# A fused attention, MLP and expert kernel: third expert chosen from six tiles, seventh tile turned on TensorE, a fourth staging buffer early

## The chip, the cores and the metric

The kernel runs on one core of one Trainium2 chip. The metric is the device time of one execution in microseconds. The kernel before took 443.18 us in the median of three runs (439.34 to 447.48). The engines are TensorE (PE, with its weight loads PEld), VectorE (DVE), ScalarE (ACT), GpSimd (POOL) and SyncE (SP), which issues most DMAs. Each works its own instructions in a fixed order.

## The reference, cut to what matters

Three stages follow each other: causal attention with a position bias, a dense MLP with `h * cos(h)`, and a mixture of eight experts with one expert per token and a capacity.

```python
x = attn_out.transpose(0, 2, 1, 3).reshape(1152, 512)   # 2 x 576 tokens
h = x @ w_in                    # 512 x 2048
x = (h * np.cos(h)) @ w_out     # 2048 x 512
logits = x @ w_gate             # 8 experts
expert_idx = np.argmax(logits, axis=1)
gate_w = probs[np.arange(N), expert_idx]          # softmax
for i in range(N):              # rows in order, up to capacity 288 each
    e = expert_idx[i]
    if counts[e] < capacity: disp[e, counts[e]] = x[i]; counts[e] += 1; keep[i] = True
h = np.maximum(np.einsum('ecd,edf->ecf', disp, w1), 0.0)   # 512 x 1024
y = np.einsum('ecf,efd->ecd', h, w2)                       # 1024 x 512
out[i] = gate_w[i] * y[expert_idx[i], pos[i]]     # kept rows, else zero
```

## The kernel before, in words

The 1152 tokens are nine tiles of 128, numbered 0 to 8. Products run as sums of fp16 parts: every operand is kept as a high and a low half, and three matmuls (high by high, high by low, low by high) make one.

The second half of the MLP (`l2_mm`, L862) first does tiles 0 to 4 together (`l2_wide`), then tiles 5 to 8 one after the other (`l2`), 48 matmuls each. When a tile is done, `l2_end` writes its two halves to `row` by ACT (L853) and DVE (L854). Each tile is then routed. `route_a` turns it: tiles below `NDT` by a DMA transpose that SP issues (L890), the others by four fp32 transposes on TensorE (L895), for which ACT first copies the tile to `xq` (L851) and afterwards copies the turned tile back (L897). `route_b` computes the logits (L912 in fp16, L909 in fp32 for the tiles turned on TensorE), takes the argmax on DVE (one-hot `roh`, L926), finds each row's place by a matmul with `tri` (L931), adds to the counts `cnt` (L941) and scatters the rows to `disp` in DRAM with an indirect DMA from POOL (L942). `l2r` interleaves all this with the matmuls of tiles 5 to 8.

The expert layer does not take the experts in order. The first is fixed. `partial` picks the next, the one with the most rows so far, and reads its number into SP's registers: once after tile `PTILE` = 4 (counts of five tiles), once after tile `HTILE` = 7 (counts of eight). The first two experts start with their first 144 rows (`HEAD`, at most; those of tiles 0 to 6), for which `hook` issues two row reads each: a transposing one to `eX` (L1008) and a small one to `eM` (L1015). After tile 8, `counts` sorts the remaining experts on DVE (L1184 to L1201) and chooses one of four tables of sizes:

```python
SIZES = (
    (64, 56, 184, 168, 152, 144, 128, 120),
    (72, 64, 192, 168, 152, 144, 136, 128),
    (88, 88, 200, 176, 160, 152, 136, 128),
    (128, 96, 216, 192, 176, 152, 144, 144),
)
```

A row must hold the rest of the first two experts, all rows of the third, and the five others by size; the program branches on that. The executed table here is the first.

Expert weights come as 64 loads of 512 KB (L964 for w1, L968 for w2; eight per expert) into staging buffers `ws`, three of them until the MLP is over and four from then on, taken in turn. Each is split by ACT (high half, L648) and then DVE (low half, L649); when DVE is done the buffer may be loaded again. `expert` computes eight steps of 12 matmuls (L1039), each into a PSUM bank of the rotation s, pt, mm with two buffers each, evicted to `eH` by ACT (L1041) and DVE (L1042), and then the second layer (L1061) and the scatter to the output (L1048). The first steps of the first expert stand beside the routing of tile 8.

What sets the order: the program records operations with their priorities, and a scheduler fixes each engine's sequence when the program is built. `after(keys, ...)` lets an operation be taken up only behind the last instruction noted under a key in `gate`: the splits wait in that sense for "ev" (the last eviction recorded) and "cnt" (the sizes).

Of the kernel before, what the change touches and what calls it, by code (L numbers as in the profile page):

```python
# [10 lines left out]
F32 = mybir.dt.float32  # L11
# [28 lines left out]
NST = 1  # L40
# [26 lines left out]
L2T = "mm"  # L67
NDT = 7
LS = 2.0 ** -11
# [5 lines left out]
def kernel(ctx, tc, q, k, v, s, w_in, w_out, wg, w1, w2, out, cap, wide):  # L75
# [19 lines left out]
    HTILE = NTILE - 2  # L95
    PTILE = PT - 1
    R0 = E - NK
    PROFILES = [[min(n, NS) for n in p] for p in SIZES]
# [748 lines left out]
    def l2_end(T, xp):  # L847
        r = work.tile([128, ROW], I32, tag="row", name="row", bufs=6)
        xf = xq[:, 0:DM] if T >= NDT else None
        if T >= NDT:  # L850
            nc.scalar.activation(xf, xp, AF.Copy, scale=2.0 ** -2)  # L851
        rh = r[:, 0:DM].bitcast(F16)
        nc.scalar.activation(rh[:, 0:DM], xp, AF.Copy, scale=2.0 ** -8)  # L853
        nc.vector.scalar_tensor_tensor(rh[:, DM:2 * DM], xp, 2.0 ** -8, rh[:, 0:DM], ALU.mult, ALU.subtract)  # L854
        nc.gpsimd.tensor_copy(r[:, DM + 1:ROW], tokid[:, T:T + 1])
        rows[T] = (r, xf)
# [29 lines left out]
    def route_a(T):  # L886
# [5 lines left out]
        else:  # L892
# [3 lines left out]
            xt = xq[:, DM:2 * DM].rearrange("p (k t) -> p k t", k=KD)  # L896
            nc.scalar.copy(xt.rearrange("p k t -> p (k t)"), tp)  # L897
            rows[T] = (r, xt)
# [55 lines left out]
    def e_weights(plan, lo=0, hi=None):  # L954
# [24 lines left out]
        for e, src, i in items:  # L979
# [5 lines left out]
            if i < KD:  # L985
                after("ev cnt", split, a[0][:, i, 0, :], a[0][:, i, 1, :], t, 64.0)
            else:
                j = (i - KD) * 2
                after("ev cnt", split, a[1][:, j:j + 2, 0, :], a[1][:, j:j + 2, 1, :], t.rearrange("p (a d) -> p a d", a=2), 64.0)
            yield  # L990
# [113 lines left out]
    def l2r(tiles, hook):  # L1104
# [5 lines left out]
        def finish():  # L1110
# [3 lines left out]
            route_b(R_)  # L1114
            if R_ in (PTILE, HTILE):
                partial()
# [92 lines left out]
    def experts(plan, group):  # L1209
# [25 lines left out]

        gate.pop("ev", None)
        gate.pop("cnt", None)

# [53 lines left out]
    with ExitStack():  # L1292
        if True:
# [6 lines left out]
            xa = early.enter_context(tc.tile_pool(name="xa", bufs=1, side="right"))  # L1300
            e_buffers(xa)
            eb["yo"] = gf[:, 4 * KF * DM:4 * KF * DM + 8 * DM].bitcast(F32).rearrange("p (i d) -> p i d", i=4)

# [19 lines left out]
            run((take(tail, lead), lead), (ahead(lead), lead))  # L1323
            ws[0:0] = [xa.tile([128, 1024], F32, name=f"ws{3 + i}") for i in range(NST)]
            phase, phase1 = (expert(h, HEAD, "out0", ex_.pop(h)) for h in range(NH))
# [54 lines left out]
```

## Time and profile before

| | |
|---|---|
| median of three runs | 443.18 us (439.34 to 447.48) |
| the profiled execution | 443.13 us, its span 441.3 us |
| mean granted clock of TensorE | 0.985 of full |
| TensorE busy | 406.3 us |
| DVE, ACT, POOL busy | 321.3, 276.9, 150.6 us |
| DMA | 77.64 MB, mean 176 GB/s |

Times in the rows count from the start of the span. A busy TensorE is not TensorE at its peak, since matmuls are pipelined. A wait for several things is put down to the one that came last by the profile. A granted clock of 1.00 is 2.4 GHz, one of 0.50 is 1.2 GHz. The second half of the MLP ends at about 299 us, the first two experts' heads run to about 335 us, and the rest to the end are the experts by the table of sizes.

### The profile page before, as it was taken

How to read it: one execution, taken by the hardware profiler on the slowest of the kernel's cores; microseconds unless marked ns; L12 is line 12 of the kernel's file. 1: busy time of each engine (PE TensorE's matmuls, PEld its weight loads, DVE VectorE, ACT ScalarE, POOL GpSimd, SP SyncE). 2: the span in 40 equal slices, each digit the busy share in tenths (PEclk: the TensorE clock that was granted, in tenths of full speed). 3: DMA queues.
4: the chain of work that ended last, by engine and by line, in shares of the span. 5: the costliest groups of instructions: out<-in, count | busy, mean ns of one | idle time of the engine just before them, and what ended most of it. 6: DMA issues, size and time to landing. Idle time of an engine off the chain costs nothing.

```text
span 441.3 us, 11029 instructions
## 1 busy us (share of the span) xinstructions
PE 406.3 (92%) x4104; PEld 294.1 (67%) x4104; DVE 321.3 (73%) x775; ACT 276.9 (63%) x642; POOL 150.6 (34%) x235
## 2 busy tenths in 40 slices
PE   2889999999999999998999999796998999889894
PEld 1677888877666665553444454355997999889862
DVE  6788999877999499889885664753822567777570
ACT  6587898995888676776224532534634577677660
POOL 7678879521454434455000032010011011122030
PEclk9999999999999999999999999998899999999898
DMA  7999894212359941232466567857568399898731
GB/s 169 199 177 194 158 172 110 64 50 81 113 183 313 336 148 55 91 95 97 143 196 229 136 134 212 266 125 241 191 191 196 98 299 250 296 315 290 257 122 48
DMA packets 91230, 77.64 MB, mean 176 GB/s; under 512 B 64006, under 2 KB 72198, under 8 KB 91167
## 3 DMA queue, kind: packets, MB, share of 16 engines
q1 hardware_dynamic: 87855, 71.85, 59.3%
q0 software_dynamic: 2256, 4.73, 3.2%
q8 instruction: 34, 0.56, 0.5%
q10 hardware_dynamic: 1056, 0.26, 0.3%
q14 instruction: 29, 0.24, 0.2%
HBM read 57.66 MB, written 12.36 MB: 159 GB/s over the span
## 4 chain that ended last, share of the span: by engine, by line
PE 30%; DMA 11%; DVE 7%; issue 5%; ACT 4%; SPq 1%; POOL 1%; ACTq 0%; POOLq 0%
DMA ws<-in_moe_w_dram 10%; PE ps_mm L862 6%; PE ps_sm L862 4%; PE ps_pt L1039 3%; PE ps_s L1039 2%; PE ps_mm L1039 2%; PE ps_pt L862 2%; PE ps_s L862 2%; PE ps_s L1061 2%; PE ps_mm L1061 2%; PE ps_pt L1061 2%; DVE gall L649 1%; ACT gall L648 1%; PE ps_mm L1078 1%; DVE y L813 1%
## 5 line engine op out<-in xcount | busy, mean ns | idle before, releaser
L807 PEld LDWEIGHTS <-win 128*128 128x128 f16 x576 | 56.2, 98 | 38.2 <-issue 1.9
L862 PEld LDWEIGHTS <-gall 128*128 128x128 f16 x432 | 40.9, 97 | 49.8 <-issue 2.4
L862 PE MATMUL ps_mm<-wout,gall 128*128 128x512 f16 x240 | 56.3, 379 | 1.3 <-DVE n__2968 L821 1.3
L649 DVE SCALAR_TENSOR_TENSOR gall<-ws,gall 128x1024 f16<-128x1024 f32 x32 | 38.9, 1222 | 24.9 <-ACT gall L648 24.0
L1048 POOL DMA_INDIRECT out_dram<-gall,eM x16 | 20.6, 1287 | 100.4 <-ACT gall L1047 92.6
L648 ACT ACTIVATE gall<-ws 128x1024 f16<-128x1024 f32 x32 | 33.9, 1059 | 26.1 <-DMA ws<-in_moe_w_dram 25.7
L240 ACT ACTIVATE z<-z,st 128x128 f32<-128x128 f32 (+3 forms) x80 | 44.3, 559 | 6.9 <-DVE st L240 6.9
L648 ACT ACTIVATE wout<-ws 128x512 f16<-128x512 f32 (+1 forms) x32 | 27.3, 861 | 26.8 <-DVE ws L671 20.5
L942 POOL DMA_INDIRECT disp<-row,rsli x9 | 9.6, 1066 | 95.5 <-ACT rm L923 48.5
L240 DVE CUSTOM_DVE_ANT_0 z<-ps_s,zm 128x512 f32<-128x512 f32 (+3 forms) x72 | 34.3, 504 | 4.5 <-PE ps_s L243 4.1
L649 DVE SCALAR_TENSOR_TENSOR wout<-ws,wout 128x512 f16<-128x512 f32 (+1 forms) x32 | 30.3, 956 | 9.7 <-ACT wout L648 9.7
L807 PE MATMUL ps_s<-xT,win 128*128 128x384 f16 x192 | 34.3, 326 | 0.0
L807 PE MATMUL ps_pt<-xT,win 128*128 128x384 f16 x192 | 33.8, 326 | 0.0
L807 PE MATMUL ps_mm<-xT,win 128*128 128x384 f16 x192 | 33.8, 326 | 0.0
L820 ACT ACTIVATE y<-y,quarter 128x384 f32<-128x384 f32 x48 | 29.3, 610 | 2.1 <-DVE y L813 2.1
L243 PE MATMUL ps_s<-kT,qT 128*128 128x128 f16 (+7 forms) x128 | 25.2, 309 | 3.5 <-DVE st L240 1.3
L1039 PEld LDWEIGHTS <-gall 128*128 128x128 f16 x480 | 27.9, 97 | 0.5 <-DVE gall L649 0.2
L649 DVE SCALAR_TENSOR_TENSOR win<-ws,win 128x1024 f16<-128x1024 f32 x16 | 19.4, 1224 | 10.9 <-ACT win L648 9.1
L246 PE MATMUL ps_pt<-idf,z 128*128 128x128 f32 x192 | 27.3, 277 | 0.1
L1061 PEld LDWEIGHTS <-gall 128*128 128x128 f16 x384 | 24.0, 101 | 3.1 <-issue 3.1
L246 PEld LDWEIGHTS ps_pt<-idf,z 128*128 128x128 f32 x192 | 21.4, 141 | 5.7 <-ACT p L240 2.8
L240 ACT COPY p<-ps_pt 128x512 f32<-128x512 f32 (+1 forms) x40 | 21.2, 562 | 4.5 <-PE ps_pt L246 4.5
(498 smaller groups left out, 921.5 us busy)
## 6 DMA issues: line engine op xcount, KB each, us to landing
ws<-in_moe_w_dram SPq DMA_DIRECT2D x64, 512.0 KB
ws<-in_moe_w_in_dram SPq DMA_DIRECT2D x16, 512.0 KB
ws<-in_moe_w_out_dram SPq DMA_DIRECT2D x16, 512.0 KB
disp<-zc SPq DMA_DIRECT2D x18, 257.0 KB
out_dram<-zc SPq DMA_DIRECT2D x9, 256.0 KB
qf<-in_q_dram SPq DMA_DIRECT2D x16, 128.0 KB
vf<-in_v_dram SPq DMA_DIRECT2D x16, 128.0 KB
kf<-in_k_dram SPq DMA_DIRECT2D x14, 128.0 KB
```

Source lines behind the costliest of these rows:

```text
L240: return pin(f(*a, **kw))
L243: return pin(nc.tensor.matmul(out_, **kw))
L246: return pin(nc.tensor.transpose(out_, in_, id_))
L648: nc.scalar.activation(hi, src, AF.Copy, scale=sc)
L649: (eng or nc.vector).scalar_tensor_tensor(lo, src, sc, hi, ALU.mult, ALU.subtract)
L807: nc.tensor.matmul(hp[:, 0:CH], lhsT=win[a][:, kk, fs], rhs=xT[:, x_, kk, xs], start=(n == 0), stop=(n == 3 * KD - 1))
L820: nc.scalar.activation(y, y, AF.Sin, scale=TWO_PI, bias=quarter)
L862: gate["pe"] = nc.tensor.matmul(xp, lhsT=G[c][:, a, f, ts], rhs=wout[w_][:, f, :], start=(f == 0 and n == 0), stop=(f == KF - 1 and n == 2))
L942: sc = nc.gpsimd.indirect_dma_start(out=disp, out_offset=bass.IndirectOffsetOnAxis(ap=sli.bitcast(U32), axis=0), in_=r, in_offset=None, bo ...
L1039: gate["pe"] = nc.tensor.matmul(hp[:, 0:ns], lhsT=a1[:, kk, a, fs], rhs=X[:, x_ * KD + kk, 0:ns], start=(n == 0), stop=(n == 3 * KD - 1))
L1048: sc = nc.gpsimd.indirect_dma_start(out=out, out_offset=bass.IndirectOffsetOnAxis(ap=M[:, b, 1:2].bitcast(U32), axis=0), in_=y, in_offset= ...
L1061: nc.tensor.matmul(yp[:, 0:ns], lhsT=a2[:, f, w_, d * 128:(d + 1) * 128], rhs=Hh[:, a, f, :], start=(n == 0), stop=(n == 3 * KE - 1))
```

## The change

Four things are changed. `partial` runs after tile 5 (`QTILE`), with counts of six tiles, instead of after tile 7. `NDT` is 6, so tile 6 is turned by TensorE like 7 and 8. The fourth staging buffer is made ahead of the loop over tiles 5 to 8 and joins the ring there. The copies to `xq` are noted under a key "xq", and the splits of expert weights are ordered behind it as well.

```diff
--- before.py
+++ after.py
@@ -65,7 +65,7 @@
 ONACT = ((1,), (2, 0), (3, 0), (3, 1))
 WT = (("sm", 2), ("sm", 2))
 L2T = "mm"
-NDT = 7
+NDT = 6
 LS = 2.0 ** -11
 BS = 64.0
 BIG = -float(2 ** 40)
@@ -94,6 +94,7 @@
     HEAD = 144
     HTILE = NTILE - 2
     PTILE = PT - 1
+    QTILE = HTILE - 2
     R0 = E - NK
     PROFILES = [[min(n, NS) for n in p] for p in SIZES]
     LIMITS = [[(n + 1) * E for n in p[NK:]] + [BIG * -1.0] * NH + [n + 1 for n in p[:NK]] for p in PROFILES]
@@ -848,7 +849,7 @@
         r = work.tile([128, ROW], I32, tag="row", name="row", bufs=6)
         xf = xq[:, 0:DM] if T >= NDT else None
         if T >= NDT:
-            nc.scalar.activation(xf, xp, AF.Copy, scale=2.0 ** -2)
+            gate["xq"] = nc.scalar.activation(xf, xp, AF.Copy, scale=2.0 ** -2)
         rh = r[:, 0:DM].bitcast(F16)
         nc.scalar.activation(rh[:, 0:DM], xp, AF.Copy, scale=2.0 ** -8)
         nc.vector.scalar_tensor_tensor(rh[:, DM:2 * DM], xp, 2.0 ** -8, rh[:, 0:DM], ALU.mult, ALU.subtract)
@@ -894,7 +895,7 @@
             for kk in range(KD):
                 nc.tensor.transpose(tp[:, kk * 128:(kk + 1) * 128], xf[:, kk * 128:(kk + 1) * 128], idf)
             xt = xq[:, DM:2 * DM].rearrange("p (k t) -> p k t", k=KD)
-            nc.scalar.copy(xt.rearrange("p k t -> p (k t)"), tp)
+            gate["xq"] = nc.scalar.copy(xt.rearrange("p k t -> p (k t)"), tp)
             rows[T] = (r, xt)
 
     def route_b(T):
@@ -983,10 +984,10 @@
             ew[e] = a
             t = pend.pop(0)
             if i < KD:
-                after("ev cnt", split, a[0][:, i, 0, :], a[0][:, i, 1, :], t, 64.0)
+                after("ev cnt xq", split, a[0][:, i, 0, :], a[0][:, i, 1, :], t, 64.0)
             else:
                 j = (i - KD) * 2
-                after("ev cnt", split, a[1][:, j:j + 2, 0, :], a[1][:, j:j + 2, 1, :], t.rearrange("p (a d) -> p a d", a=2), 64.0)
+                after("ev cnt xq", split, a[1][:, j:j + 2, 0, :], a[1][:, j:j + 2, 1, :], t.rearrange("p (a d) -> p a d", a=2), 64.0)
             yield
 
     ex_ = {}
@@ -1112,7 +1113,7 @@
             if R_ == HTILE:
                 hook()
             route_b(R_)
-            if R_ in (PTILE, HTILE):
+            if R_ in (PTILE, QTILE):
                 partial()
 
         for T in tiles:
@@ -1233,8 +1234,8 @@
                 next(feed)
                 state["fed"] += 1
 
-        gate.pop("ev", None)
-        gate.pop("cnt", None)
+        for key in ("ev", "cnt", "xq"):
+            gate.pop(key, None)
 
         def adv(e, k):
             if e >= n:
@@ -1299,6 +1300,7 @@
             run((l2_wide(range(WN), seq(wo, take(pre, items + 1)), L2F), KF + 1))
             xa = early.enter_context(tc.tile_pool(name="xa", bufs=1, side="right"))
             e_buffers(xa)
+            ws[0:0] = [xa.tile([128, 1024], F32, name=f"ws{3 + i}") for i in range(NST)]
             eb["yo"] = gf[:, 4 * KF * DM:4 * KF * DM + 8 * DM].bitcast(F32).rearrange("p (i d) -> p i d", i=4)
 
             def hook():
@@ -1321,7 +1323,6 @@
             tail = l2r(range(WN, NTILE), hook)
             lead = (NTILE - WN) * KF // 2 + 1
             run((take(tail, lead), lead), (ahead(lead), lead))
-            ws[0:0] = [xa.tile([128, 1024], F32, name=f"ws{3 + i}") for i in range(NST)]
             phase, phase1 = (expert(h, HEAD, "out0", ex_.pop(h)) for h in range(NH))
             for _ in range(RF):
                 next(phase)
```

Line numbers of the kernel after are one higher from the second line of the diff on: its L965 is L964 of before. Three places show what moved.

SP's issues around the row reads of the first two experts (`eX`, `eM`; `ws_...` are the staging buffers, `psi` the chosen expert's number). Before:

```order
L968 DMA ws_93<-in_moe_w_dram 128x2x512
L1008 DMA_TRANSPOSE eX<-disp 128x8x144
L1015 DMA eM_3457<-disp 72x2x2
...
L1015 DMA eM_3458<-disp 72x2x2
L1165 TENSOR_LOAD psi
L1165 ISA x2
L964 ISA
L964 DMA ws_91<-in_moe_w_dram 128x1024
```

After:

```order
L969 DMA ws_3465<-in_moe_w_dram 128x2x512
L1166 TENSOR_LOAD psi
L1166 ISA x2
L969 ISA
L969 DMA ws_92<-in_moe_w_dram 128x2x512
...
L969 DMA ws_93<-in_moe_w_dram 128x2x512
L1009 DMA_TRANSPOSE eX<-disp 128x8x144
L1016 DMA eM_3457<-disp 72x2x2
...
L1016 DMA eM_3458<-disp 72x2x2
L969 ISA
L969 DMA ws_91<-in_moe_w_dram 128x2x512
```

The third expert's number is read within the second expert's loads, and seven of the third expert's eight loads stand ahead of the row reads; before, all eight stood behind them.

ACT around the copies of tile 8 (`xq`, `row`), the splits (`gall<-ws_...`) and the first evictions of the first expert (`eH`). Before:

```order
L648 ACTIVATE gall<-ws_91 128x1024
L851 ACTIVATE xq<-ps_mm 128x512
L853 ACTIVATE row<-ps_mm 128x512
L648 ACTIVATE gall<-ws_92 128x1024
L897 COPY xq<-ps_pt 128x512
L648 ACTIVATE gall<-ws_93 128x1024
L1041 ACTIVATE eH<-ps_s 128x144
```

After:

```order
L649 ACTIVATE gall<-ws_91 128x1024
L933 ACTIVATE rex,rm<-ps_s,rm 128x8
L852 ACTIVATE xq<-ps_mm 128x512
L854 ACTIVATE row<-ps_mm 128x512
L898 COPY xq<-ps_pt 128x512
L1042 ACTIVATE eH<-ps_s 128x144
L1042 ACTIVATE eH<-ps_pt 128x144
L649 ACTIVATE gall<-ws_3465 128x2x512
```

The split ahead of the copy was the first of the third expert's eight and is now the fourth; none stands between the two copies.

DVE at the end of the sizes (`ov`, `fl`), with the third expert's last four splits and the evictions of the first expert. Before:

```order
L1198 TENSOR_TENSOR ov<-ky,limit 1x10 x4
L1042 SCALAR_TENSOR_TENSOR eH<-ps_mm,eH 128x144
L1199 TENSOR_REDUCE ky<-ov 1x4
L1042 SCALAR_TENSOR_TENSOR eH<-ps_s,eH 128x144
L1201 TENSOR_REDUCE fl<-ky 1x1
L649 SCALAR_TENSOR_TENSOR gall<-ws_92,gall 128x2x512
```

After:

```order
L1199 TENSOR_TENSOR ov<-ky,limit 1x10 x4
L1200 TENSOR_REDUCE ky<-ov 1x4
L1202 TENSOR_REDUCE fl<-ky 1x1
L650 SCALAR_TENSOR_TENSOR gall<-ws_3465,gall 128x2x512
L650 SCALAR_TENSOR_TENSOR gall<-ws_92,gall 128x2x512
L650 SCALAR_TENSOR_TENSOR gall<-ws_93,gall 128x2x512
L650 SCALAR_TENSOR_TENSOR gall<-ws_91,gall 128x2x512
L1043 SCALAR_TENSOR_TENSOR eH<-ps_mm,eH 128x144
```

All eight evictions of the first expert, and two of the second, stood among or ahead of the operations of the sizes, so ahead of the four splits of w2; now those from the first expert's third step on stand behind these four splits.

## Rows read from the trace of the kernel before

**Rows 1.** The page, parts 1 and 4: busy us and share by engine; chain's shares.

```profile
PE 406.3 (92%) x4104; PEld 294.1 (67%) x4104; DVE 321.3 (73%) x775; ACT 276.9 (63%) x642; POOL 150.6 (34%) x235
...
PE 30%; DMA 11%; DVE 7%; issue 5%; ACT 4%; SPq 1%; POOL 1%; ACTq 0%; POOLq 0%
```

**Rows 2.** Windows, start:end and length, then busy us by engine, PEclk, DMA share, GB/s.

```profile
270.00:300.00 30.00, 27.10 (x158) 13.23 (x155) 16.56 (x53) 11.95 (x21) 3.92 (x6) 1.00 0.72 199
300.00:314.00 14.00, 10.44 (x110) 10.24 (x108) 7.50 (x21) 8.28 (x18) 0.48 (x1) 0.76 0.82 275
```

**Rows 3.** Timeline of TensorE, 271 to 317 us: start, duration, engine, line; idle before in brackets.

```profile
271.04 6.85 PE L862 MATMUL ps_mm<-wout,gall 128*128 128x512 f16 x31
...
282.20 0.46 PE L912 MATMUL ps_s<-wgs,xr 128*128 128x8 f16 x12 [2.75 <-ACT gall L648]
...
291.90 0.96 PE L909 MATMUL ps_s<-wg_sb,xq 128*128 128x8 f32 x8
...
294.11 0.17 PE L1155 MATMUL ps_sm<-cnt,onesm 128*128 128x8 f16 x1
...
299.31 0.91 PE L1039 MATMUL ps_s<-eX,win 128*128 128x144 f16 x12
303.79 0.65 PE L895 MATMUL ps_pt<-idf,xq 128*128 128x128 f32 x4 [3.56 <-ACT xq L851]
...
313.75 0.91 PE L1039 MATMUL ps_mm<-eX,gall 128*128 128x144 f16 x12
...
316.75 1.66 PE L1061 MATMUL ps_s<-eH,win 128*128 128x144 f16 x24
```

**Rows 4.** Waits of the whole span: total us, times, longest.

```profile
PEld L912 <- DMA xr<-row: 3.2, 1, 3.2
```

**Rows 5.** Timeline of SP's issues, 270 to 346 us.

```profile
270.18 6.98 SPq L964 DMA_DIRECT2D ws<-in_moe_w_dram  x4
277.43 1.27 SPq L890 DMA_TRANSPOSE xr<-row  x1
...
292.61 1.30 SPq L1008 DMA_TRANSPOSE eX<-disp  x1
...
298.40 6.46 SPq L964 DMA_DIRECT2D ws<-in_moe_w_dram  x4
...
332.90 12.93 SPq L1008 DMA_TRANSPOSE eX<-disp  x3
```

**Rows 6.** Timeline of ACT, 274 to 304 us.

```profile
274.49 1.06 ACT L648 ACTIVATE gall<-ws 128x1024 f16<-128x1024 f32 x1 [3.53 <-DMA ws<-in_moe_w_dram]
...
302.19 1.06 ACT L648 ACTIVATE gall<-ws 128x1024 f16<-128x1024 f32 x1 [8.41 <-DMA ws<-in_moe_w_dram]
303.15 0.58 ACT L851 ACTIVATE xq<-ps_mm 128x512 f32<-128x512 f32 x1
```

**Rows 7.** Timeline of DVE, 275 to 322 us.

```profile
275.57 1.23 DVE L649 SCALAR_TENSOR_TENSOR gall<-ws,gall 128x1024 f16<-128x1024 f32 x1 [3.58 <-ACT gall L648]
...
291.31 1.23 DVE L649 SCALAR_TENSOR_TENSOR gall<-ws,gall 128x1024 f16<-128x1024 f32 x1 [1.17 <-ACT gall L648]
...
313.94 0.15 DVE L1184 SCALAR_TENSOR_TENSOR ky<-ps_sm,keys 1x8 f32<-1x8 f32 x1 [0.50 <-PE ps_sm L1177]
...
316.86 0.13 DVE L1201 TENSOR_REDUCE fl<-ky 1x1 int32<-1x4 f32 x1
316.92 4.61 DVE L649 SCALAR_TENSOR_TENSOR gall<-ws,gall 128x1024 f16<-128x1024 f32 x4
321.47 0.29 DVE L1042 SCALAR_TENSOR_TENSOR eH<-ps_pt,eH 128x144 f16<-128x144 f32 x1
```

**Rows 8.** Timeline of POOL at the scatter of tile 7.

```profile
299.50 0.97 POOL L942 DMA_INDIRECT disp<-row,rsli  x1 [8.91 <-DMA eM<-disp]
```

**Rows 9.** Windows of two stretches at the lower clock.

```profile
304.90:311.60 6.70, 6.70 (x55) 6.70 (x53) 4.22 (x12) 4.13 (x11) 0.00 (x0) 0.50 0.65 210
410.70:414.00 3.30, 3.30 (x31) 3.30 (x29) 1.88 (x4) 2.63 (x5) 0.00 (x0) 0.50 0.89 305
```

## Prediction

> **What bounds the kernel now.** I read the busy times first: TensorE is busy 92% of the span, and the chain that ended last is 30% TensorE's with 11% in DMA [rows 1]. So time is to be had only where TensorE idles or is slow, and the change touches one such place, the second half of the second MLP and the start of the expert layer. The windows show it: of 270 to 300 us TensorE is busy 27.10 of 30 at full clock, of 300 to 314 us only 10.44 of 14 at a mean clock of 0.76 [rows 2]. The timeline then names the holes [rows 3]: 2.75 us ahead of the logits of tile 6 at 282.20, and 3.56 us ahead of the transposes of tile 8 at 303.79.
>
> The first hole is blamed on an ACT split, but the weight-load side of the same instruction waited 3.2 us for the transposed rows, a DMA [rows 4]. SP shows why they were late: the transpose of tile 6 went out at 277.43, behind the fourth of four weight loads that starts at 276.8 because it wants a staging buffer back [rows 5]. The second hole is ACT's: a split waited 8.41 us for its load and went first at 302.19; the copy of tile 8, which TensorE needed, followed at 303.15 [rows 6]. That load was the first of the third expert, issued only at 298.40 [rows 5], since the expert is chosen from eight tiles. The reader is to see that both holes are queue order, not lack of bandwidth.
>
> **The tail of the second MLP (271 to 299 us).** The change takes the transpose of tile 6 off SP: minus 2.75 us of idle. TensorE gets four transposes (0.65 us, the row at 303.79) and fp32 logits (0.96 us, the row at 291.90) in place of fp16 ones (0.46 us, at 282.20): plus 1.15 [rows 3]. Two small waits come new. The transposes of tile 6 stand 19 matmuls behind 271.04, at 0.221 us each (6.85 over 31) at 275.2, but on ACT the copy that feeds them stands behind the first split of the second expert, which begins at 274.49 when its load lands; a split holds ACT 0.96 us (302.19 to 303.15) and the copy takes 0.58 [rows 3, 6]. It ends at 276.0: plus 0.8. Then DVE's one-hot of tile 6 now stands behind the fifth split. That load goes out when the first split is done (275.57 + 1.23 = 276.8 [rows 7]), lands 4.3 later as the first one did (270.18 to 274.49 [rows 5, 6]), and 1.06 of ACT and 1.23 of DVE put the one-hot at about 283.9; TensorE, after 0.65, 12 matmuls, 0.96 and 14 matmuls, is there at about 283.2: plus 0.8 rounded up. Sum: -2.75 + 1.15 + 0.8 + 0.8 = 0. The tail ends where it did, at 299.3.
>
> **What the fourth buffer and the earlier choice do.** With three buffers eight splits went by from 275.57 to 291.31, 2.25 us apiece [rows 7]. Each buffer's round thus took 6.75 us; four share the same round at 1.69. DVE was busy 16.56 of the 30 us to 300 [rows 2], so four more splits of 1.23 fit (21.5). At 1.69 the eleventh split ends at 276.8 + 16.9 = 293.7. That is when the fifteenth load goes out, and the third expert's loads are in early: their split no longer holds the copy of tile 8 on ACT. So the hole of 3.56 us at that place goes.
>
> **What is moved past what.** SP is one queue. The row reads of the first two experts (two transposes, two small reads), issued at 292.61, are now behind seven loads of the third expert. They go out at about 293.7 + 0.6 = 294.3. The nearest price is the transpose of tile 6: issued 277.43, used at 282.20, 4.77 us with a load ahead of it [rows 3, 5]. So the first rows land at 299.1, and TensorE asks at 299.3: no wait taken; the lower end is zero, the upper end stands with the rivals. The eighth load, behind those reads, goes out near 298.6 and lands 4.3 later, at 302.9; its ACT split is wanted only by DVE's last split near 309, so it hides. POOL's scatter of tile 7 waited for those small reads (8.91 us, to 299.50 [rows 8]); it will go at about 301.5, and the scatter of tile 8 behind it is ready only after 303.7, so this too is covered.
>
> **From 299.3 to the second expert's first step.** Ten matmuls of the first expert at 0.0625 us (48 in 313.75 to 316.75 [rows 3]) 0.6; transposes of tile 8 0.65; copy 0.6: logits start at 301.2. From logits to new counts took 291.90 to 294.11, 2.2 us [rows 3], and one eviction (0.29 [rows 7]) is now among those DVE operations: 303.7. The sizes follow 0.2 us later; on DVE they ran from 313.94 to 316.92, 2.98 us, with six evictions at a pitch of some 0.22 between them [rows 7], which now stand elsewhere: 1.7 us, so 305.6. And here a new wait takes the place of the old one. DVE then runs the last four splits of the third expert in one block, 4.61 us as at 316.92 [rows 7], to 310.2, and only behind them stands the eviction (0.29) of the first expert's third step. The second expert's first step takes that PSUM bank. TensorE has done the 53 matmuls left of the first expert's steps by 303.7 + 53 x 0.0625 = 307.0 and stands until 310.5. Before, this step began at 313.75 [rows 3]. Net: -3.25 us.
>
> **After that** the instructions stand in the same order on all engines. Nothing gives the 3.25 us back that I can see: SP's reads and loads for the later experts are held by TensorE's own progress (three transposes take 12.93 us from 332.90 [rows 5]), so the stream shifts with it, and the sizes reach SP about 10 us earlier, more than TensorE gains.
>
> The profiled execution took 443.13 us, its span 441.3 and 1.8 around it; the median of the runs is 443.18. So 443.13 - 3.25 = **439.9 us**.
>
> **Rivals.**
> (1) The clock falls in the new hole. In the row of 304.9 to 311.6 the granted clock is 0.50, 1.2 GHz of 2.4, after the idle of 3.56 us, and once more from 410.7 to 414.0 [rows 3, 9]; the 2.75 us ahead of 282.20 cost nothing, the clock stayed 1.00 to 300 [rows 2]. The new hole is 3.5 us. Half of 3.3 or of 6.7 us is lost: +1.65 to +3.35, that is 441.6 to 443.3. For it: 3.5 us is near 3.56. Against it: of two holes of about this size only one was followed by the lower clock, and the work on both sides of the new one is dense. Chance 0.25.
> (2) The row reads come late, and the kernel is slower. If the fourth buffer doesn't speed the splits and they go on at 2.25 us, the eleventh ends at 299.3, the reads go out at 299.9 and land at 304.7: TensorE waits 5.4 us at 299.3, 443.13 - 3.25 + 5.4 = 445.3, and with a slow stretch of 6.7 us 448.6. It decides above 2.04 us per split: there the wait is 3.25 and the gain is gone. For it: the row chains of two tiles and the splits share DVE. Against it: DVE's spare time. A milder form keeps 1.69: the fifteenth load, out at 293.8, lands 4.3 later at 298.1, and the transposed rows start only then; without the 1.27 us of issue they take up to 3.5 more, 301.6, which makes 442.2. The Trainium skill (DMA: Bandwidth & Descriptors, Queues, rings and completion order) speaks for this form: descriptors on one ring are consumed in order, so a transfer issued behind loads starts behind them; the row of 4.77 us, with one load ahead, doesn't tell two loads' worth apart from none. Chance 0.22 for both.
> (3) More goes than I count: the two waits of 0.8 us in the tail don't come, 438.3; with everything gone that was lost there, 2.75 + 3.56 and the half of 6.7, it would be 433.5. The DVE block of 4.61 us speaks against the second. Chance 0.12.
> (4) The choice comes out otherwise: with another third expert, a larger one stays among the sorted rest and the next table of sizes is taken, 64 columns more in sum; 192 matmuls per column set at 3.0 us per 48 of 144 columns make 5.3 us more, 445.2. The reference's own inputs, counted after six and after eight tiles, give the same expert (121 and 150 rows, the most of those left). Chance 0.02.
>
> **Numbers.** The forecast keeps 0.39. It is 439.9; the two tail waits and the row wait put 438.3 to 440.8 around it. The range takes in rival 1, the mild form of 2 with part of the harsh one, and most of 3: 435.5 to 446.5. The runs shown lie from 439.34 to 447.48, so 2%, 8.9 us, is about what can be told from no change. Faster by that needs nearly all of rival 3's larger form: 0.08. Slower by it needs more than rival 2's 448.6: 0.04. The rest, 0.88.
>
> **What would show it.** Right: no idle ahead of tile 6's logits beyond 1 us; tile 8's copy on ACT directly at the end of the MLP; four splits in a row on DVE from about 305.6, and TensorE idle until they end, near 310.5. Rival 1 shows as a granted clock of 0.50 after that; rival 2 as an idle ahead of the first expert's first matmul, released by the transposed rows. The prediction is wrong if the splits run slower than 2.04 us apiece, or if TensorE meets the DVE block without idling.

## The result and the profile after

The changed kernel takes 445.75 us in the median of 21 runs (442.06 to 450.78), the kernel before, beside it, 443.16 us (438.35 to 447.48, 21 runs). The ratio, taken from the fast runs alone (16 of the change's 21), is 1.0103, with an interval of 1.0071 to 1.0135: the change costs 3.1 to 6.0 us, more than the 2.6 by which the medians of all runs differ, and both profiled executions of the change (449.83 and 449.91 us) took longer than any of these 16. The forecast was 439.9. The time lies in the stated range and within 2% of the kernel before, but on the other side of it than the forecast.

The page of after, parts 1 and 4. Beside [rows 1], TensorE is as busy and the chain has the same shape: the shares don't show what went wrong.

```profile
PE 406.8 (91%) x4104; PEld 294.3 (66%) x4104; DVE 323.8 (72%) x775; ACT 278.1 (62%) x644; POOL 151.0 (34%) x235
...
PE 29%; DMA 12%; DVE 7%; ACT 5%; issue 4%; POOL 2%; SPq 0%; ACTq 0%; POOLq 0%; DVEq 0%
```

The profiled execution took 449.83 us, and it is 4.35 us behind the one before already at tile 5's logits (273.62 against 269.27), in stages that the change does not touch. So the two are compared from there to the first expert's second layer (L1062, L1061 before): 47.48 us before [rows 3], forecast 44.23, and now 49.64. Tile 5's logits before, then after:

```profile
269.27 0.45 PE L912 MATMUL ps_s<-wgs,xr 128*128 128x8 f16 x12
```

```profile
273.62 0.45 PE L913 MATMUL ps_s<-wgs,xr 128*128 128x8 f16 x12
```

The same stretch in the timeline of TensorE, after. Columns as in [rows 3]; line numbers are larger by one.

```profile
280.02 0.66 PE L896 MATMUL ps_pt<-idf,xq 128*128 128x128 f32 x4 [0.64 <-ACT xq L852]
...
288.09 0.17 PE L932 MATMUL ps_sm<-roh,tri 128*128 128x16 f16 x1 [0.94 <-DVE rm L939]
...
301.37 0.17 PE L932 MATMUL ps_sm<-roh,tri 128*128 128x16 f16 x1 [1.22 <-DVE rm L939]
...
306.53 0.79 PE L1040 MATMUL ps_s<-eX,win 128*128 128x144 f16 x10 [1.74 <-DMA eX<-disp]
...
310.82 0.17 PE L1177 MATMUL ps_sm<-cnt,onesm 128*128 128x8 f16 x1
...
318.62 0.91 PE L1040 MATMUL ps_mm<-eX,gall 128*128 128x144 f16 x12 [4.28 <-DVE eH L1043]
319.37 1.56 PE L1040 MATMUL ps_s<-eX,gall 128*128 128x144 f16 x12
...
323.26 1.66 PE L1062 MATMUL ps_s<-eH,win 128*128 128x144 f16 x24
```

The two holes of before (2.75 and 3.56 us) are gone. In their place stand five waits, 8.82 us together. Behind the longest, the same 12 matmuls take 1.56 instead of 0.91 us.

The windows of after, as [rows 2], and one over the second expert's steps behind the hole:

```profile
270.00:300.00 30.00, 28.41 (x176) 14.67 (x175) 21.07 (x69) 16.96 (x30) 5.64 (x6) 1.00 0.85 288
300.00:314.00 14.00, 11.04 (x128) 8.79 (x127) 7.33 (x46) 7.33 (x19) 1.82 (x2) 1.00 0.74 150
319.30:323.20 3.90, 3.90 (x40) 3.90 (x38) 1.26 (x5) 0.87 (x3) 0.00 (x0) 0.56 0.35 64
```

To 300 us DMA moves 288 GB/s instead of 199: the fourth buffer and the earlier choice work. TensorE gains nothing by it. It looks busier in this window only because the execution is 4.35 us late and its third wait lies behind 300: up to the end of the second MLP its idle is 2.80 us (0.64, 0.94 and 1.22), before 2.75. Behind that end it is 6.02 us (1.74 and 4.28), before 3.56.

SP's issues and the timelines of ACT and DVE tell where the waits come from. SP of after, as [rows 5]:

```profile
295.36 4.25 SPq L969 DMA_DIRECT2D ws<-in_moe_w_dram  x3
299.65 1.30 SPq L1009 DMA_TRANSPOSE eX<-disp  x1
```

The first expert's rows are asked for at 299.65, directly behind three loads, and TensorE has them at 306.53, 6.88 us later. The row that the forecast used, with one load ahead, was 4.77.

ACT of after at tile 8's copy, as [rows 6]:

```profile
304.83 0.60 ACT L852 ACTIVATE xq<-ps_mm 128x512 f32<-128x512 f32 x1 [4.67 <-PE ps_mm L863]
```

The copy now goes as soon as TensorE is done with the tile; no split holds it.

DVE of after, as [rows 7]:

```profile
299.94 1.23 DVE L650 SCALAR_TENSOR_TENSOR gall<-ws,gall 128x1024 f16<-128x1024 f32 x1 [0.40 <-ACT gall L649]
301.09 0.23 DVE L927 TENSOR_SCALAR roh<-rw,rm 128x8 f16<-128x8 f32 x1
...
311.05 0.15 DVE L1185 SCALAR_TENSOR_TENSOR ky<-ps_sm,keys 1x8 f32<-1x8 f32 x1
...
313.67 0.15 DVE L1202 TENSOR_REDUCE fl<-ky 1x1 int32<-1x4 f32 x1
313.75 4.61 DVE L650 SCALAR_TENSOR_TENSOR gall<-ws,gall 128x1024 f16<-128x1024 f32 x4
318.28 0.29 DVE L1043 SCALAR_TENSOR_TENSOR eH<-ps_mm,eH 128x144 f16<-128x144 f32 x1
```

At 301.09 tile 7's one-hot comes behind a split, and TensorE waits 1.22 us for it. At 313.75 the four splits run in a row, and the eviction that TensorE needs follows at 318.28.

### The profile page after: what moved, and what is told of

It is laid out like the page before. It is cut to its first block, busy times and chain, and to the rows that moved or that the text cites. A ratio compares the mean times of both kernels' runs of the same rounds, so it can differ in the third digit from the quotient of the medians.

```text
span 448.1 us, 11037 instructions
## 1 busy us (share of the span) xinstructions
PE 406.8 (91%) x4104; PEld 294.3 (66%) x4104; DVE 323.8 (72%) x775; ACT 278.1 (62%) x644; POOL 151.0 (34%) x235
## 4 chain that ended last, share of the span: by engine, by line
PE 29%; DMA 12%; DVE 7%; ACT 5%; issue 4%; POOL 2%; SPq 0%; ACTq 0%; POOLq 0%; DVEq 0%
DMA ws<-in_moe_w_dram 10%; PE ps_mm L863 6%; PE ps_sm L863 4%; PE ps_s L1062 3%; PE ps_s L1040 2%; PE ps_pt L1040 2%; PE ps_mm L1040 2%; PE ps_pt L863 2%; PE ps_s L863 2%; ACT gall L649 2%; DVE gall L650 2%; PE ps_mm L1062 2%; PE ps_pt L1062 2%; POOL gall L830 2%; DMA eX<-disp 2%
## 5 line engine op out<-in xcount | busy, mean ns | idle before, releaser
L863 PEld LDWEIGHTS <-gall 128*128 128x128 f16 x432 | 41.0, 98 | 51.9 <-issue 4.7
L943 POOL DMA_INDIRECT disp<-row,rsli x9 | 10.0, 1111 | 88.6 <-ACT rm L924 48.5
L1040 PEld LDWEIGHTS <-gall 128*128 128x128 f16 x480 | 29.7, 101 | 5.6 <-issue 4.9
L247 PE MATMUL ps_pt<-idf,z 128*128 128x128 f32 x192 | 28.7, 285 | 0.7 <-DVE p L241 0.6
L247 PEld LDWEIGHTS ps_pt<-idf,z 128*128 128x128 f32 x192 | 22.5, 146 | 6.7 <-ACT p L241 2.3
L1062 PEld LDWEIGHTS <-gall 128*128 128x128 f16 x384 | 23.8, 101 | 3.0 <-issue 3.0
```

The costliest lines, as they stand in the source:

```text
L247: return pin(nc.tensor.transpose(out_, in_, id_))
L863: gate["pe"] = nc.tensor.matmul(xp, lhsT=G[c][:, a, f, ts], rhs=wout[w_][:, f, :], start=(f == 0 and n == 0), stop=(f == KF - 1 and n == 2))
L943: sc = nc.gpsimd.indirect_dma_start(out=disp, out_offset=bass.IndirectOffsetOnAxis(ap=sli.bitcast(U32), axis=0), in_=r, in_offset=None, bo ...
L1040: gate["pe"] = nc.tensor.matmul(hp[:, 0:ns], lhsT=a1[:, kk, a, fs], rhs=X[:, x_ * KD + kk, 0:ns], start=(n == 0), stop=(n == 3 * KD - 1))
L1062: nc.tensor.matmul(yp[:, 0:ns], lhsT=a2[:, f, w_, d * 128:(d + 1) * 128], rhs=Hh[:, a, f, :], start=(n == 0), stop=(n == 3 * KE - 1))
```

## The theories, and the experiments

Theory A: the earlier choice puts work of the third expert in front of what TensorE needs next, above all the four splits in a row ahead of the first expert's evictions; the gain is given back there, and the clock falls behind the hole. Theory B: the difference is chance, falls of the clock in stages that the change does not touch. Theory C: a wait taken away at one place comes back at the next, whatever is edited.

All kernels but the repeats were timed in five rounds beside the kernel before (12 runs each, 6 for e3, e4 and e8; medians of before 442.0 in the first four, 443.25 in the next four, 442.96 in the last). For each profile the table gives the stretch named above (tile 5's logits to the second layer), split into TensorE's idle, the time that the granted clock took (windows of 1 us, length times one minus the granted clock), and the rest, which is work:

| kernel | stretch | idle | clock | rest | ratio to before |
|---|---|---|---|---|---|
| before | 47.48 | 6.31 | 3.42 | 37.75 | |
| before, again | 44.76 | 5.29 | 1.71 | 37.76 | |
| the change | 49.64 | 8.82 | 1.70 | 39.12 | 1.0103 [1.0071, 1.0135] |
| the change, again | 52.84 | 9.05 | 5.12 | 38.67 | |
| e1, splits spread | 46.84 | 6.21 | 1.71 | 38.92 | 0.994 [0.9901, 0.9979] |
| e2, choice late | 46.63 | 5.90 | 1.70 | 39.03 | 1.0022 [0.9987, 1.0057] |
| e12, two splits | 46.75 | 7.35 | 0.00 | 39.40 | 1.0038 [0.9995, 1.008] |
| e3, tile 6 by DMA | 54.01 | 11.40 | 5.13 | 37.48 | 1.021 [1.0128, 1.0293] |
| e4, three buffers | 54.53 | 10.63 | 5.12 | 38.78 | 1.0161 [1.0076, 1.0247] |
| e5, reads early | 52.32 | 8.37 | 5.12 | 38.83 | 1.0096 [1.0062, 1.0129] |
| e6, spread and early | 46.83 | 4.78 | 3.41 | 38.64 | 0.9973 [0.9932, 1.0014] |
| e8, spread, by DMA | 47.05 | 7.53 | 1.70 | 37.82 | 1.0109 [1.0042, 1.0176] |
| e8, again | 51.42 | 6.98 | 8.53 | 35.91 | |
| e10, one split out | 41.85 | 2.57 | 0.00 | 39.28 | 0.9919 [0.9871, 0.9966] |

In "e8, again" 2.9 us of the low clock lie within idle time and are counted in both columns, so its rest comes out 1.5 us low.

The span and the mean granted clock of each run behind a ratio give the same split for whole executions (means, good to about half a us): with the change the clock took 5.9 us and the span without it is 437.6, in the three sets of runs of the kernel before 5.3 to 5.6 and 433.5 to 434.7. So most of the loss is idle and work, and the clock adds under 1 us. The two numbers are 3.6 and 433.2 for e1, 3.9 and 438.2 for e12, 4.7 and 434.0 for e6, 8.1 and 435.6 for e8, 2.8 and 432.4 for e10.

**The four splits (e1).** The loop that asks for four splits behind the counts is taken out; the scheduler then takes them up among the evictions.

```diff
             regs = counts()
-            for _ in range(KE // 2):
-                next(pre)
             order, first = registers(*regs)
```

> The kernel after, without the loop that takes the last four splits of the third expert right behind the sizes; they are taken between the steps of the first two experts instead, so five evictions of the first expert stand ahead of them on DVE. Theory A (the gain was given back at the DVE block of 4.6 us and by the lower clock behind it): the idle of 4.28 us ahead of the second expert's first step falls under 0.5 us, the granted clock stays 1.00 there, and the time falls by 4 to 6 us against the kernel after, to 440 to 442 us. Rival B (the kernel after is slower by chance of the clock in stages that the change doesn't touch): the idle may go, but the time stays at that of the kernel after within 1 us. Rival C (the splits only move their wait): the idle comes back as a wait of the first expert's second layer for the eighth eviction, 3 us or more, and the time falls by less than 1.5 us.

Measured: 439.27 us (434.43 to 445.28, 12 runs), below the 440 to 442 expected and faster than the kernel before. TensorE of e1 at the rows' wait and at the second expert's first step, then DVE:

```profile
303.85 1.36 PE L1040 MATMUL ps_s<-eX,win 128*128 128x144 f16 x10 [2.62 <-DMA eX<-disp]
...
313.10 0.91 PE L1040 MATMUL ps_mm<-eX,gall 128*128 128x144 f16 x12
```

```profile
312.87 0.31 DVE L1043 SCALAR_TENSOR_TENSOR eH<-ps_s,eH 128x144 f16<-128x144 f32 x1
313.10 0.13 DVE L1202 TENSOR_REDUCE fl<-ky 1x1 int32<-1x4 f32 x1
313.16 3.48 DVE L650 SCALAR_TENSOR_TENSOR gall<-ws,gall 128x1024 f16<-128x1024 f32 x3
```

Five evictions now stand among the sizes, ahead of three splits in a row; TensorE meets no block at 313.10, and nothing comes back at the third expert. The clock stays full there; its one fall in the stretch stands behind the rows' wait of 2.62 us. This is for A at that place, and against B and C: 1.0103 becomes 0.994 by an order of work on ACT and DVE alone. Of what e1 wins on the change, 4.4 us are idle and work (437.6 and 433.2) and 2.3 the clock.

**Half of it (e12).** Two splits are asked for there, not four.

```diff
-            for _ in range(KE // 2):
+            for _ in range(KE // 4):
                 next(pre)
```

> The change as timed, but only two of the third expert's last splits are asked for right behind the counts, not four. Theory A (what blocks is the run of splits on DVE that stands ahead of the first expert's evictions): three evictions now stand ahead of the first split, so the idle of 4.28 us at the second expert's first step falls to 1.5 us or less, and the clock does not fall behind it; the wait of 1.7 to 2.6 us for the first expert's rows stays: 440 to 442.5 by fast runs, 0 to 0.7% under the kernel before. Rival (the idle there has another cause, such as the sizes on DVE): 444 to 447, with an idle of 3 us or more there.

Measured: 443.71 us (440.2 to 450.04), more than expected. The idle at the place is between that of four and of none, and larger than the 1.5 us expected:

```profile
315.20 0.91 PE L1040 MATMUL ps_mm<-eX,gall 128*128 128x144 f16 x12 [2.30 <-DVE eH L1043]
```

DVE of e12 at that place:

```profile
310.32 4.61 DVE L650 SCALAR_TENSOR_TENSOR gall<-ws,gall 128x1024 f16<-128x1024 f32 x4
```

Four splits still run in a row, as in the change. What the edit moves is the evictions: three now stand among the sizes ahead of the block, none in the change, and six in the kernel before, where the same block of 4.61 us [rows 7] makes no hole. So the hole (4.28, 2.30, none) follows the evictions that stand ahead of the block; a shorter block was not tried alone, since e1 has five evictions ahead and three splits in a row. The clock held in the stretch, as expected, but in this execution it fell twice later, at 379.6 and 413.7 us (1.7 us each). In the time the dose does not show so well: the ratio is between those of e1 and the change, its interval takes in no change, and without the clock e12's span is as long as the change's (438.2 and 437.6). What else is long in e12 is open.

**The choice itself (e2).** The third expert is chosen after tile 7 again; the rest of the change stays.

```diff
-            if R_ in (PTILE, QTILE):
+            if R_ in (PTILE, HTILE):
```

> The kernel after with one part undone: the third expert is again chosen from eight tiles, so its loads stand behind the row reads, and the evictions stand among the sizes as in the kernel before. Tile 6 on TensorE and the early fourth buffer stay. Theory A: the wait for the row reads (1.9 us) and the DVE block's idle (4.3 us) are both gone, the wait for the third expert's first load comes back at tile 8 unless the order of the copies avoids it; time between 440 and 444 us, 2 to 5 us under the kernel after. Rival B: same time as the kernel after within 1 us.

Measured: 441.98 us (439.92 to 445.28), no difference from before. The old hole at tile 8's copy is back, the wait for the rows and the hole at the block are gone. TensorE of e2:

```profile
305.51 0.76 PE L896 MATMUL ps_pt<-idf,xq 128*128 128x128 f32 x4 [3.91 <-ACT xq L852]
...
314.28 0.91 PE L1040 MATMUL ps_mm<-eX,gall 128*128 128x144 f16 x12
```

So it is the earlier choice that brings the loads and splits into the way, and the three other edits alone neither win nor lose.

**The wait for the rows (e5, e6).** The row reads are issued one tile earlier, ahead of the last loads; in e6 together with e1's edit.

```diff
         def finish():
             R_ = mid.pop(0)[0]
-            if R_ == HTILE:
-                hook()
             route_b(R_)
+            if R_ == HTILE - 1:
+                hook()
```

> The kernel after with the row reads of the first two experts issued behind the routing of tile 6 instead of ahead of the routing of tile 7: they stand ahead of five of the third expert's loads on SP, not behind seven. Same rows are read. Theory A: the first expert's first matmul no longer waits for the transposed rows (1.7 to 1.9 us in the kernel after, under 0.3 here), the DVE block and its idle stay; time 1 to 2.5 us under the kernel after. Rival B: the loads held up behind the reads make the splits late, TensorE waits 1 to 2 us more for a one-hot, and the time stays or rises.

> Both edits: the row reads behind the routing of tile 6, and the last four splits between the experts' steps. Theory A: both waits gone; 6 to 8 us under the kernel after, at 438 to 440 us, so faster than the kernel before by 3 to 5 us. Rival B (clock by chance): within 1 us of the kernel after. Rival C (the waits only move): between 442 and 445 us.

Measured: 445.93 us (442.79 to 447.89) and 440.76 (437.38 to 444.91). The rows' wait is gone in both, and nothing is won: e5 takes as long as the change, e6 misses its 438 to 440 and is not faster than e1. ACT and then TensorE of e5:

```profile
302.52 1.06 ACT L649 ACTIVATE gall<-ws 128x1024 f16<-128x1024 f32 x1 [6.02 <-DMA ws<-in_moe_w_dram]
303.48 0.58 ACT L852 ACTIVATE xq<-ps_mm 128x512 f32<-128x512 f32 x1
```

```profile
304.12 0.66 PE L896 MATMUL ps_pt<-idf,xq 128*128 128x128 f32 x4 [2.43 <-ACT xq L852]
...
318.03 1.33 PE L1040 MATMUL ps_mm<-eX,gall 128*128 128x144 f16 x12 [3.70 <-DVE eH L1043]
```

The load that the reads now precede lands late, its split holds ACT until 303.48, and tile 8's copy stands behind it: the old hole, 2.43 us. For this wait theory C is right.

**That split taken away too (e10).** As e6, and the third expert's fourth split is no longer asked for within the second MLP.

```diff
-                    if i > KF // 2 + 1 and k < min(len(P["o"]) * items, 2 * items + KD):
+                    if i > KF // 2 + 1 and k < min(len(P["o"]) * items, 2 * items + KD - 1):
```

> No four splits in a row, the row reads one tile earlier, and the third expert's fourth split taken out of the second MLP (its load is the one that stood behind the row reads and held the copy of tile 8 on ACT for 2.3 us). Theory A (each of these waits is a queue order, and can be taken away without coming back): no wait for the rows, idle ahead of tile 8's transposes under 0.8 us, no idle of over 1 us at the second expert's first step: about 2 us under the version with both but without this, 438 to 439, and under 442.0 for the kernel before. Rival C (the waits only move, to the third expert's late splits): 440 to 441.5, with an idle of 1.5 us or more at the third expert's first step or at the second layer of the first two.

Measured: 437.68 us (434.14 to 443.98, 12 runs), the lowest median here, 0.9919 of before, though its interval overlaps those of e1 and e6. TensorE of e10:

```profile
299.14 0.79 PE L1040 MATMUL ps_s<-eX,win 128*128 128x144 f16 x10
299.99 0.66 PE L896 MATMUL ps_pt<-idf,xq 128*128 128x128 f32 x4
...
307.07 0.91 PE L1040 MATMUL ps_mm<-eX,gall 128*128 128x144 f16 x12
...
317.87 0.48 PE L1069 MATMUL ps_pt<-idf,xq 128*72 128x128 f32 x2 [1.53 <-ACT xq L1064]
```

No wait for rows, none at tile 8, none at the second expert; the stretch is 41.85 us, 4.98 shorter than in e6, with the clock at full throughout. Of the 4.98 us, 3.41 are the clock, which in e6's profile fell behind its hole of 2.32 us, and 2.21 are idle, less 0.64 more work. The split that was moved does come back, behind the stretch, as an idle of 1.53 us at 317.87 in the second layer of the first expert, the sign that C named. So C takes back 1.5 of the 2.2 us of idle, and what stays won is mostly clock: 2.8 us a run, against 5.3 in the kernel before beside it, while the spans without the clock (432.4 and 433.5) are not told apart.

**Tile 6 by DMA again (e3, e8).** In the change as timed, and in e1.

```diff
-NDT = 6
+NDT = 7
```

> The change as timed, but tile 6 is turned by DMA again (NDT = 7). Theory A (the change loses its gain at the wait for the first expert's rows and at DVE's block of four splits): the idle of 2 to 3 us ahead of tile 6's logits comes back and the 1.15 us of fp32 work goes, so TensorE reaches the end of the second MLP 1 to 1.5 us later than with the change, but it waits 1.74 us there for the rows anyway, and the wait shrinks to under 0.8 us; the DVE block and its idle of about 4 us stay: 445 to 447, within 0.3% of the change as timed. Rival (the turning by TensorE is itself what costs): 443.5 or less, with the idle of 1.7 us or more still there ahead of the first expert.

> The version without the four splits in a row (439.27 before), with tile 6 turned by DMA again. Theory A: there the wait for the first expert's rows was 2.62 us, so 1 to 1.5 us more in the tail is swallowed by it: 439 to 440, the wait ahead of the first expert down to 1.2 to 1.6 us. Rival (the tail's end sets the time): 440.5 to 441.5, with the wait unchanged near 2.6 us.

Measured: 450.19 us (447.2 to 453.64) and 445.54 (444.06 to 446.52). Both expectations failed: they said that the rows' wait would swallow a later tail; it grew instead, to 3.41 and 3.63 us. SP of e3, then POOL:

```profile
287.14 0.34 SPq L965 DMA_DIRECT2D ws<-in_moe_w_dram  x1
287.53 1.60 SPq L891 DMA_TRANSPOSE xr<-row  x1
...
305.96 1.30 SPq L1009 DMA_TRANSPOSE eX<-disp  x1
```

```profile
300.95 1.31 POOL L943 DMA_INDIRECT disp<-row,rsli  x1 [23.39 <-ACT rex L933]
```

Tile 6's transpose stands behind a load that waits for its buffer, so its scatter goes at 300.95 (290.93 in the change), and the reads, which need the rows that it writes, at 305.96 (299.65). Turning tile 6 on TensorE costs 1.15 us of work by the forecast and is worth more than that, through the scatter and the row reads, which the sum left out: the ratios of e8 and e1 lie clearly apart (those of e3 and the change just touch). In the stretch of e8 alone it doesn't show (47.05 against 46.84 in e1), so e8 was profiled once more.

> The version without the four splits in a row and with tile 6 turned by DMA, profiled once more. In its first profile the stretch from tile 5's logits to the second layer took 47.05 us, as long as with tile 6 turned by TensorE (46.84), and yet the six runs lay 1.5% above that version. Theory A (more falls of the clock behind the waits that it adds): the stretch is 47 to 50 us, and the granted clock is 0.50 for 3 us or more at two places or more between 290 and 420 us. Rival B (the stages ahead): tile 5's logits at 271 us or later again, and at most one such place.

Measured: the stretch is 51.42 us, above the 47 to 50 of A, and two windows of it lie near half clock:

```profile
289.00:297.00 8.00, 6.49 (x31) 3.18 (x32) 4.00 (x10) 6.04 (x10) 0.00 (x0) 0.57 1.02 325
306.00:318.00 12.00, 8.91 (x79) 8.91 (x79) 3.71 (x28) 3.28 (x11) 1.23 (x2) 0.57 0.44 115
```

The first goes with an idle of 2.97 us ahead of tile 7's transposes; in e8's first profile that idle was 2.61 us, and the clock held. The second goes with an idle of 3.36 us for the rows. So A's cause, and a part of B's condition with it: tile 5's logits start at 271.37 here and 271.28 there. Over its six runs the clock took 8.1 us, in e1's 3.6, which is more than half of what e8 loses to e1. How much of e8's 1.09% lies in the stages ahead is open.

**The fourth buffer (e4).** It comes after the second MLP, as before.

```diff
-            ws[0:0] = [xa.tile([128, 1024], F32, name=f"ws{3 + i}") for i in range(NST)]
             eb["yo"] = ...
...
             run((take(tail, lead), lead), (ahead(lead), lead))
+            ws[0:0] = [xa.tile([128, 1024], F32, name=f"ws{3 + i}") for i in range(NST)]
```

> The change as timed, but the fourth staging buffer comes only after the second MLP, where it came before. Theory A: the row reads go out earlier among the loads, so the wait for the first expert's rows is under 0.5 us; splits go by at about 2.25 us each, so the split ahead of tile 8's copy on ACT is late again and TensorE idles 2 to 4 us there; the block of four splits and its idle of 3 to 4.5 us stay, as does the lower clock behind it: 445 to 447.5. Rival (the fourth buffer, by putting seven loads ahead of the row reads, is what costs): 443 or less, with no idle over 1 us between 295 and 308 us.

Measured: 447.63 us (446.05 to 452.21), just above the 445 to 447.5 expected. The rows come without a wait, as A expected, and the block's hole stays (4.29 us). The third wait was expected at tile 8's copy on ACT; it stands one tile earlier and on DVE, where tile 7's one-hot is behind late splits:

```profile
302.86 0.17 PE L932 MATMUL ps_sm<-roh,tri 128*128 128x16 f16 x1 [4.32 <-DVE roh L927]
```

So the fourth buffer is not what costs. That it is worth its place is not shown by the ratios, 1.0161 and 1.0103, whose intervals overlap.

**Chance (r1_after, r1_before).** The change and the kernel before, profiled once more on one chip.

> The change as timed, profiled once more. Its first profile stood 4.35 us behind that of the kernel before at tile 5's logits, in stages that the change does not touch, 1.7 of them by one fall of the clock at 36 us. Theory A (chance of that execution): tile 5's logits start between 268 and 271.5 us, and from there to the second layer of the first expert it takes 49 to 50.5 us again. Rival B (the changed kernel is slower there always): 273 us or later, with waits for the transposed keys in the first 60 us that add up to 3 us more than in the kernel before.

> The kernel before, profiled once more, on the same chip as the change. Theory A: tile 5's logits between 268 and 272 us, from there to the second layer 46.5 to 48.5 us. Rival B: within 0.5 us of 269.3 at tile 5's logits, and 3 us or more ahead of the change there.

Measured: tile 5's logits at 270.48 and 271.38 us, so the 4.35 us of the first pair was chance and B's always-slower stage falls. The stretches missed on both sides, 52.84 against 49 to 50.5, and 44.76 against 46.5 to 48.5, and in both the clock's share moved most, as the table shows (5.12 and 1.71 us, in the first pair 1.70 and 3.42). The change, again, TensorE and two windows:

```profile
304.15 0.79 PE L1040 MATMUL ps_s<-eX,win 128*128 128x144 f16 x10 [2.44 <-DMA eX<-disp]
...
318.69 1.45 PE L1040 MATMUL ps_mm<-eX,gall 128*128 128x144 f16 x12 [3.76 <-DVE eH L1043]
```

```profile
304.00:312.00 8.00, 7.85 (x70) 7.84 (x70) 2.44 (x20) 5.12 (x10) 0.97 (x1) 0.58 0.37 119
318.69:322.57 3.88, 3.88 (x36) 3.88 (x36) 1.64 (x7) 0.58 (x2) 0.00 (x0) 0.56 0.50 104
```

Here the clock fell behind the rows' wait too. Without the clock the stretch is 44.06 and 43.05 us before, 47.94 and 47.72 after: 4.3 us more, of which 3.1 are idle (mean of 8.82 and 9.05 against 6.31 and 5.29) and 1.1 work. That is inside the 3.1 to 6.0 us by which the runs differ.

The fourth edit, the splits ordered behind the rows' copies, was not run alone: without it the instructions of all engines stand in the same order, so it does nothing here.

## Why the prediction was wrong, step by step

| step | forecast | measured (twice) |
|---|---|---|
| wait ahead of tile 6's transposes | 0.8 | 0.64, 0.75 |
| wait for tile 6's one-hot | 0.8 | 0.94, 1.19 |
| wait for tile 7's one-hot | none | 1.22, 0.91 |
| wait for the first expert's rows | 0 | 1.74, 2.44 |
| TensorE idle at the DVE block | 3.5 | 4.28, 3.76 |
| fp32 work of tile 6 | 1.15 | 1.4, 0.9 (what the table's rest grew by) |
| clock in the stretch (before 3.42, 1.71) | 0 | 1.70, 5.12 |

Two steps of the sum failed: the clock's 3.42 us were counted as won, and "no wait taken" for the row reads, with tile 7's one-hot left out and the hole at the block too short, put the idle 3.7 us too low (3.95 in the second pair). The first leaves no gain, the second makes the loss. Neither of the two signs of being wrong that the prediction named came true (splits at 1.85 us, TensorE idle at the block), so the signs were too narrow. Rival 4 did not come: the first table of sizes runs here too.

- **The tail** was right to within 0.4 us in each of its four terms, and the idle ahead of tile 6's logits went. Missed, at 1.22 and 0.91 us, was that tile 7's one-hot meets a split on DVE as tile 6's does: with 12 splits by then instead of 8 the same reasoning had to be used twice.
- **"No wait taken" for the row reads failed.** The splits went by at 1.85 us (279.52 to 297.98 for ten), not 1.69: that puts the reads 1.4 us later. And the price of 4.77 us was of a transpose with one load ahead; with three, it was 6.88. The mild form of rival 2 had this mechanism and gave 301.6, a wait of 2.3. The Trainium skill (DMA: Bandwidth & Descriptors, Queues, rings and completion order) had spoken for it: the descriptors of one ring are taken in order. The trace agrees in the direction (6.88 against 4.77 us). So do the other runs: the same read took 6.2 to 7.3 us from issue to use where a load had been issued within 0.5 us ahead of it (the change twice, e1, e12) and 3.4 where none had for 5 us (e3 and e8 twice; in e4 to landing). No run moved the loads alone, and e2's read took 5.1 us to landing with no load for 10 us, so loads are not all of it.
- **The DVE block** was right as a mechanism: four splits directly behind the sizes, TensorE idle until the eviction. The hole was 0.8 and 0.3 us longer than the 3.5 forecast. The sizes took 2.77 us, not 1.7: where I took six evictions out of them, six operations of tile 8's scatter (L935 to L941) came in.
- **The clock, rival 1, is where the forecast gain was lost.** Idle and work of the forecast add up to what they were before (5.1 + 1.15 against 6.31). The whole gain of 3.25 us was the 3.42 us that the clock had taken behind the hole of 3.56 us [rows 9], and I let it go with that hole while putting one of 3.5 us in its place. It fell behind the new hole both times. And the kernel before loses 3.42 us of it in one execution and 1.71 in the next, so a row of one execution was no price to be won back. The clock alone does not make the change slower, though: over the runs it took about as much as before (5.9 us and 5.3 to 5.6). The loss is the idle that the sum left out. The prediction counted one of two holes of that size as followed by a fall. The trace of before has a third, right ahead of the second stretch of [rows 9], so it was two of three:

```profile
410.40 2.84 PE L1061 MATMUL ps_mm<-eH,gall 128*128 128x144 f16 x24 [2.78 <-DVE eH L1042]
```

- **"Nothing gives the 3.25 us back" after the second layer** held in the first pair: from there to the end it took 124.84 us, against 124.55 before. In the second pair it took 124.88 against 122.46, of which 1.71 is a fall of the clock at 387 us. Whether a part of the rest is the change's is open.
- Rivals 1 and 2 came together. I had priced them one at a time, each against a full gain. Both at once give 439.9 + 1.65 + 2.3 = 443.8, and with tile 7's one-hot (1.1) and the longer hole (0.5) 445.4, near the median of 445.75.

## What to carry to other kernels

Before a hole is counted as gained, list what the same queue will do next: here loads, splits and evictions share SP, ACT and DVE in strict order, and work that comes earlier stands in front of something that TensorE needs. Take the time that a low clock cost out of the sum first, and forecast idle and work without it; then ask of each new hole whether the clock may fall behind it. When the new order is right in one place, try the next place as well: the same change with the splits spread, the reads earlier and one split less is 0.8% faster than before, most of it because the clock falls less, where the change alone is 1.0% slower. And a run of splits is not bad in itself: count what stands ahead of it, here the evictions that give TensorE work for as long as the run lasts.

## What the runs showed of the hardware that was not expected

The clock's price came in steps: each fall to 0.50, 1.2 GHz of 2.4, took about 1.7 us or a multiple of it, and ahead of the last 10 us of the span a profile holds from none (e10) to four (e3) of them. The length of an idle did not tell alone. At the later experts an idle of 3.15 us (e6, 410.41 us) was followed by full clock, and one of 2.12 us (the change, again, 386.34 us) by a fall; at the rows' wait 2.62 us (e1) was followed by a fall and 1.74 us (the change) not. Behind the block's hole of 3.70 to 4.35 us the clock fell in all five profiles that have it; behind e12's of 2.30 us it held. Two profiles of the same kernel differ by 2.7 to 4.4 us in one stretch of 50, in the kernel before 1.7 of 2.7 by the clock. And the stages ahead of it, which no edit touches, brought tile 5's logits to anywhere between 268.2 and 273.6 us.
